# A sparse-attention and mixture-of-experts kernel: the gating's VectorE instructions regrouped, and scatters freed from an early read

## The chip, the cores and the metric
One core of one Trainium2 chip runs the whole program. The metric is device time in microseconds of an execution, as the median of several runs. Engines named here: TensorE (PE), VectorE (DVE), ScalarE (ACT), GpSimd (Pool), and SyncE (SP), which here only issues DMAs.

## The reference
Inputs q, k, v have the shape 8 x 8 x 576 x 64 (batch, head, position, feature). In heads 0 to 3 a query sees the last 32 positions up to itself; in heads 4 to 7 it sees the earlier positions of the same residue modulo 32. Scores are scaled, shifted by their row maximum, exponentiated, normalised and multiplied with v. The result is reshaped to 4608 tokens of 512 features and goes through a top-1 mixture of 8 experts:

```
logits = x @ w_gate;  e = argmax(logits);  p = softmax(logits)[e]
s = sigmoid(x @ w_output_gate)[e]
out[token] = p * s * (relu(x @ w1[e]) @ w2[e])      # w1: 512x1024, w2: 1024x512
```

## The kernel before, in words
**Stages.** Attention runs first, in 40 steps: 8 batches (b) of 5 steps (j = 0 to 4, step t = 5b + j), a step being one tile of queries of all the heads it concerns. Then comes a drain of some 20 short turns, and then the experts, one after the other, each with two layers of matmuls in a split fp32 form.

**The pipeline of a step.** The loop at the end of `attention` writes the order of the instructions by hand; each engine executes its own in that order. Step t holds: scores of tile t on PE; normalisation of tile t-4 on DVE in three instructions (`norm`, lines 345, 347, 350, the last of which writes x_t); the DMA stores of x_t and the loads of later inputs on SP; masking (`bar`) and row maximum (`top`, line 291) of tile t on DVE; transposes of tile t-2 on PE and their copy on ACT; the product with the values for tile t-3 on PE (`values`); the subtraction of the maximum on Pool (`shift`, line 306), one instruction of 128x512; transposes of x_t (`turn_x`), their copy in the next step (`evac_x`, ACT); the exponential on ACT (`expo`). `even` copies half of the local values to a shifted tile (vev), one half of the partitions on DVE and one on ACT, twice a batch, at j = 3 and j = 4 after the row maximum.

**The gating.** While batch b+1 is in attention, batch b is gated. `logits` (two halves of 288 tokens) multiplies x with both gate matrices in four strips of PE (line 413), copies to SBUF on ACT (line 417), transposes on PE (line 422) and adds the four strips on DVE (line 424). `gating` then works on tiles of 96 partitions x 6 x 8: row maximum, difference, tie-break, one-hot `oh`, its bf16 copy `ohb` (line 535), the chosen output logit, a running count of tokens per expert by triangular matmuls on PE (lines 544 to 549), the sum with the expert's base address (line 560), the product with `oh` (line 565) and its sum, the slot number as an integer (line 574), the weight (line 572). Six scatters (line 581) on Pool write token number and weight to a table in DRAM, one for each 96 tokens. Batch 7 is gated in two halves (3 scatters each), so there are nine gatings.

**The pump.** Gating and logits are generators. `pump` is called eight times a step; each call moves a generator on to its next `yield`. `yield n` makes it pass over n calls. In the drain a call goes on as long as yields are 0, in the steps it makes one move.

**The early read.** After the gating of batch 3 the kernel picks the expert with most tokens (`pick`), reads the first 256 rows of its table (`ahead`, line 470, a DMA from Pool's queue), fetches these tokens' rows by an indirect DMA on Pool and loads that expert's w1 through SP. In the drain `lead_layer` computes that expert's first layer for them on PE, one matmul at a time between the gating's work, with PSUM released by ACT (line 504) and DVE (line 506). At the end `rank` orders the experts on DVE (lines 436 to 446).

The scatters are declared free of one another (`distinct`); the framework derives every other wait from the memory that instructions read and write, the table in DRAM among it. Tiles named gp in PSUM have two buffers for all of: logits, transposes, counts, `pick`, `rank`.

## Time and profile before
| | |
|---|---|
| median of 3 runs | 645.34 us (643.64 to 649.53) |
| profiled execution | 644.6 us, of which the span of instructions is 643.0 us |
| busy: PE, DVE, ACT, Pool | 607.0, 307.2, 262.9, 188.6 us |
| DMA | 96.34 MB, mean 150 GB/s |
| mean granted clock of PE | 0.991 of 2.4 GHz |
| chain that ended last | PE 72%, issue 11%, DVE 7%, DMA 3%, ACT 3%, Pool 2% |

Busy times are means over stages that differ: the attention is the first quarter of the span, and there DVE is busy eight to nine tenths of each slice; in the experts PE is busy nine tenths and more, and DVE two to four. A time such as 63.55 is counted from the start of the span.

### The profile page before, as it was taken

The numbers are of one execution on the slowest core, as the hardware profiler recorded it, in microseconds if no ns is written. First come the engines' busy times: TensorE is split into PE (matmuls) and PEld (weight loads), VectorE is DVE, ScalarE is ACT, GpSimd is POOL, SyncE is SP. The second block draws the span as 40 slices with busy tenths as digits, with TensorE's granted clock in tenths as the row PEclk, the third lists the DMA queues.
The fourth block names the chain that finished last, engine by engine and source line by source line (L and its number), as shares of the span: only waits on it lengthen the run. The fifth ranks groups of instructions, "written<-read, shape, count | busy, mean of one in ns | idle before, by whom it ended". The sixth has DMA issues, their size and how long they took to land.

```text
span 643.0 us, 14884 instructions
## 1 busy us (share of the span) xinstructions
PE 607.0 (94%) x5909; PEld 517.0 (80%) x5909; DVE 307.2 (48%) x685; ACT 262.9 (41%) x519; POOL 188.6 (29%) x194
## 2 busy tenths in 40 slices
PE   7889898878899999999999999999999999999995
PEld 5666666656578889978998899889879988988983
DVE  4888999967672243332243234236333432532500
ACT  3766665547262153333332333243233333433410
POOL 4327555675455015011401130132015014011011
PEclk9999999979999999999999999999999999999998
DMA  8989898893524535054306342245154064161000
GB/s 315 322 283 286 286 291 274 259 340 86 181 69 135 184 103 169 1 174 143 116 2 209 125 159 67 92 126 167 35 150 129 7 208 145 36 213 48 1 22 36
DMA packets 45537, 96.34 MB, mean 150 GB/s; under 512 B 8898, under 2 KB 20438, under 8 KB 45466
## 3 DMA queue, kind: packets, MB, share of 16 engines
q1 hardware_dynamic: 36010, 71.95, 34.8%
q0 software_dynamic: 8048, 20.05, 9.6%
q10 hardware_dynamic: 1408, 3.38, 1.5%
q8 instruction: 47, 0.77, 0.5%
q14 instruction: 24, 0.20, 0.1%
HBM read 75.85 MB, written 20.35 MB: 150 GB/s over the span
## 4 chain that ended last, share of the span: by engine, by line
PE 72%; issue 11%; DVE 7%; DMA 3%; ACT 3%; POOL 2%; SPq 0%; POOLq 0%; DVEq 0%; ACTq 0%
PE hp L810 29%; PE yp L830 28%; PE tp L800 3%; PE sp L499 2%; PE yp L854 2%; PE xtp L381 2%; PE xp L332 1%; PE sp L259 1%; DVE st L291 1%; PE tp L317 1%; DVE p_t L277 1%; POOL out_dram L874 1%; PE sp L264 1%; POOL p_t L306 1%; ACT xt L396 1%
## 5 line engine op out<-in xcount | busy, mean ns | idle before, releaser
L810 PE MATMUL hp<-xh,w1l 128*128 128x256 f32 (+1 forms) x480 | 147.9, 308 | 0.0
L810 PE MATMUL hp<-xl,w1h 128*128 128x256 f32 (+1 forms) x480 | 147.8, 308 | 0.0
L810 PE MATMUL hp<-xh,w1h 128*128 128x256 f32 (+1 forms) x480 | 147.7, 308 | 0.0
L874 POOL DMA_INDIRECT out_dram<-ys,tab x36 | 38.3, 1064 | 248.9 <-ACT ys L873 237.8
L810 PEld LDWEIGHTS hp<-xh,w1h 128*128 128x128 f32 x480 | 91.0, 190 | 1.9
L810 PEld LDWEIGHTS hp<-xl,w1h 128*128 128x128 f32 x480 | 91.0, 190 | 1.9
L810 PEld LDWEIGHTS hp<-xh,w1l 128*128 128x128 f32 x480 | 90.9, 189 | 1.4
L739 DVE TENSOR_TENSOR xl<-tp,xh 128x512 fp32r<-128x512 f32 (+3 forms) x40 | 25.6, 649 | 103.3 <-ACT xh L738 103.3
L818 DVE SCALAR_TENSOR_TENSOR hlb<-hp,hhb 128x384 fp32r<-128x384 f32 (+3 forms) x64 | 33.0, 516 | 85.5 <-ACT hf L817 43.2
L815 ACT ACTIVATE hhb<-hp 128x384 fp32r<-128x384 f32 (+3 forms) x64 | 29.3, 458 | 102.8 <-PE hp L810 97.9
L830 PE MATMUL yp<-w2h,hhb 128*128 128x512 f32 (+1 forms) x176 | 71.0, 404 | 0.0
L830 PE MATMUL yp<-w2l,hhb 128*128 128x512 f32 (+1 forms) x176 | 69.6, 395 | 0.0
L830 PE MATMUL yp<-w2h,hlb 128*128 128x512 f32 (+1 forms) x176 | 69.1, 393 | 0.0
L738 ACT CAST xh<-tp 128x512 fp32r<-128x512 f32 (+3 forms) x40 | 21.8, 556 | 114.4 <-PE tp L800 114.4
L306 POOL TENSOR_TENSOR p_t<-p_t,st 128x512 f32<-128x512 f32 x40 | 46.1, 1154 | 60.0 <-DVE cum L557 16.6
L830 PE MATMUL yp<-w2h,hha 128*128 128x512 f32 x128 | 51.4, 401 | 0.0
L581 POOL DMA_INDIRECT table<-meta,dst x48 | 44.5, 927 | 22.0 <-issue 10.2
L830 PE MATMUL yp<-w2l,hha 128*128 128x512 f32 x128 | 50.2, 393 | 0.0
L830 PE MATMUL yp<-w2h,hla 128*128 128x512 f32 x128 | 50.1, 392 | 0.0
L818 DVE SCALAR_TENSOR_TENSOR hla<-hp,hha 128x256 fp32r<-128x256 f32 x56 | 23.6, 421 | 54.9 <-ACT hha L815 54.9
L155 POOL DMA_INDIRECT xg<-xd,tab x40 | 44.4, 1109 | 15.4 <-issue 12.7
L310 ACT ACTIVATE p_t<-p_t 128x512 f32<-128x512 f32 x40 | 25.2, 631 | 57.1 <-POOL p_t L306 56.9
(151 smaller groups left out, 1036.8 us busy)
## 6 DMA issues: line engine op xcount, KB each, us to landing
raw<-in_moe_w_dram SPq DMA_DIRECT2D x54, 512.0 KB
vst<-in_vs_dram SPq DMA_DIRECT2D x8, 780.0 KB
vlt<-in_vl_dram SPq DMA_DIRECT2D x16, 292.5 KB
q_t<-in_ql_dram SPq DMA_DIRECT2D x8, 576.0 KB
q_t<-in_qs_dram SPq DMA_DIRECT2D x7, 650.0 KB
xd<-x_t SPq DMA_DIRECT2D x80, 54.0 KB
xd<-x_t SPq DMA_DIRECT2D x16, 256.0 KB
raw<-in_moe_w_dram ACTq DMA_DIRECT2D x6, 512.0 KB
```

The costliest lines, as they stand in the source:

```text
L155: nc.gpsimd.indirect_dma_start(out=dst, out_offset=None, in_=src, in_offset=bass.IndirectOffsetOnAxis(ap=idx, axis=0), bounds_check=top, o ...
L306: nc.gpsimd.tensor_tensor(out=p_t, in0=p_t, in1=st, op=ALU.subtract)
L310: nc.scalar.activation(out=p_t, in_=p_t, func=AF.Exp, scale=scale)
L581: i = nc.gpsimd.indirect_dma_start(out=table[:, :], out_offset=bass.IndirectOffsetOnAxis(ap=dst[:, j:j + 1], axis=0), in_=meta[:, b * NB + ...
L738: nc.scalar.copy(out=hi, in_=src)
L739: nc.vector.tensor_tensor(out=lo, in0=src, in1=f32(hi), op=ALU.subtract)
L800: nc.tensor.transpose(out=tv[:, k, 0:m], in_=xg[0:m, 128 * k:128 * (k + 1)], identity=ident[0:m, 0:m])
L810: nc.tensor.matmul(out=hp[:, 0:n], lhsT=w[:, k, 128 * j:128 * (j + 1)], rhs=x[:, k, 0:n], start=first, stop=(k == KC - 1 and w is w1l))
L815: nc.scalar.activation(out=hh[:, j, 0:s], in_=hp[:, 0:s], func=AF.Relu)
L818: nc.vector.scalar_tensor_tensor(out=hl[:, j, 0:s], in0=hp[:, 0:s], scalar=0.0, in1=f32(hh[:, j, 0:s]), op0=ALU.max, op1=ALU.subtract)
L830: nc.tensor.matmul(out=yp[0:m, :], lhsT=h[:, j, o:o + m], rhs=w[:, j, :], start=(j == 0 and q == 0), stop=(j == FC - 1 and q == 2))
L874: i = nc.gpsimd.indirect_dma_start(out=out.rearrange("t (k d) -> (t k) d", k=k), out_offset=bass.IndirectOffsetOnAxis(ap=row, axis=0), in_ ...
```

## The change
- `logits`: the transposes and DVE's sum are replaced by a matmul with a matrix of zeros and ones (`fold`, new columns of ecst) that transposes and adds in one, and a copy on ACT.
- `gating`: `oh` is written as bf16 at once; the base addresses are added by the counting matmul, through two more rows of `cum` (filled by one small ACT copy at step 3); the sum of the slot numbers is written as an integer directly. The order is new.
- `pump` has a ninth call, number 9, between normalisation and masking, and a yield can name the call by number. For batches 0 to 5 the gating's instructions that read two tensors from SBUF are at call 9 (`MID`), its reductions at calls 3 to 6; for batches 6 and 7 the yields are counts as before, all of them 0 within `gating`.
- `even`: DVE's copies stand between normalisation and masking, at j = 4 and at j = 0 of the next batch (for batch 7 both at j = 4); ACT's stay before the exponential of these steps.
- The scatters are declared independent of the early read. `pick` and the transposes of `ahead` are tied to calls.

```diff
-                nc.vector.tensor_reduce(
-                    out=ls[b][:, HB * hf:HB * (hf + 1), :],
-                    in_=lv.rearrange("p j (c e) -> p j e c", c=KC)[:, :, 0:2 * E, :], axis=AX.X, op=ALU.add)
-                yield 0
+                    nc.tensor.matmul(out=lv[:, j, :], lhsT=lg[:, QB * j:QB * (j + 1)], rhs=fold, start=True, stop=True)
+                yield spot(b, 1, 1)
+                nc.scalar.copy(out=ls[b][:, HB * hf:HB * (hf + 1), :], in_=lv)
+                yield spot(b, 1, 5)
...
+                yield spot(b, 0, MID)
+                oh = gt.tile([QB, n, E], BF16, name="oh")
                 nc.vector.tensor_tensor(out=oh, in0=ew, in1=bc(f[:, 1, :]), op=ALU.is_equal)
-                yield 0
-                ohb = gt.tile([QB, n, E], BF16, name="ohb")
-                nc.vector.tensor_copy(out=ohb, in_=oh)
-                yield 0
-                nc.vector.tensor_tensor(out=dd[:, 0], in0=oh, in1=l[:, :, E:2 * E], op=ALU.mult)
+                nc.vector.tensor_tensor(out=dd[:, 2], in0=oh, in1=l[:, :, E:2 * E], op=ALU.mult)
+                yield spot(b, 0, 3)
...
+                nc.tensor.matmul(out=pv, lhsT=tri[0:QB + 2, 1, 0:QB],
+                                 rhs=cum[:, ci, :].unsqueeze(1).to_broadcast([QB + 2, n, E]), start=False, stop=False)
...
-                nc.vector.tensor_tensor(out=dd[:, 0], in0=pv.rearrange("p (j e) -> p j e", j=n),
-                                        in1=ec(ebase), op=ALU.add)
...
-                nc.vector.tensor_tensor(out=dd[:, 0], in0=dd[:, 0], in1=oh, op=ALU.mult)
...
-                nc.vector.tensor_reduce(out=f[:, 6, :], in_=dd[:, 0], axis=AX.X, op=ALU.add)
...
-                nc.vector.tensor_copy(out=dst, in_=f[:, 6, :])
+                yield spot(b, 0, MID)
+                nc.vector.tensor_tensor(out=cum[0:QB, ci + 1, :], in0=cum[0:QB, ci, :], in1=s8, op=ALU.add)
...
+                yield spot(b, 0, 3)
+                dst = dpool.tile([QB, n], I32, name="dst")
+                nc.vector.tensor_tensor(out=dd[:, 0], in0=pv.rearrange("p (j e) -> p j e", j=n), in1=oh, op=ALU.mult)
+                yield spot(b, 0, 4)
+                    nc.vector.tensor_reduce(out=dst, in_=dd[:, 0], axis=AX.X, op=ALU.add)
...
                     distinct(i, scatters)
+                    for r in early:
+                        tc.declare_no_dep(i.ins, r.ins, reason="the slots read were all given by earlier batches")
                     yield 3
...
-            def pump():
+            def pump(at=None):
                 clock[0] += 1
                 k = clock[0]
                 for c in chains:
-                    if k >= c[1]:
+                    if at in c[2] if at and c[2] else k >= c[1]:
...
-                pump()
+                pump(1)
                 at(norm, 4, 1)
-                pump()
+                pump(2)
                 at(norm, 4, 2)
...
+                pump(9)
+                shifted = ((0, 1) if b == B - 1 else (0,)) if j == 4 else (1,) if b and j == 0 else ()
+                for h in shifted:
+                    even(t // NS - (j == 0), nc.vector, h, 0)
                 at(bar, 0)
```

The scatters of a batch start three calls after the weight's reciprocal, and follow each other every fourth call (`yield 3`), before as after.

## Rows read from the trace of the kernel before

**Rows 1.** Windows, cut at the shift's starts of steps 5, 10, 21, 26, 33, 39.

```profile
core 0: us, PE busy (x) PEld busy (x) DVE busy (x) ACT busy (x) POOL busy (x), PEclk, DMA share, GB/s
...
23.13:39.64 16.51, 15.77 (x383) 12.04 (x384) 13.38 (x28) 12.90 (x27) 5.82 (x6) 1.00 0.93 306
...
81.91:100.48 18.57, 16.28 (x391) 12.46 (x391) 17.05 (x49) 11.55 (x26) 11.18 (x12) 1.00 0.90 283
...
127.64:153.83 26.19, 22.60 (x478) 17.61 (x471) 20.28 (x55) 14.45 (x33) 16.55 (x16) 0.87 0.75 259
153.83:198.40 44.57, 38.60 (x301) 29.32 (x300) 29.15 (x96) 20.88 (x41) 21.72 (x22) 1.00 0.34 106
```

**Rows 2.** Chain that ended last, steps 26 and 27: start, us, what.

```profile
100.69 0.91 DVE ohb L535
...
104.92 5.34 DMA hla<-in_kl_dram
```

**Rows 3.** VectorE's groups in 81.91 to 100.48: count, busy us, mean ns, idle before.

```profile
L565 DVE TENSOR_TENSOR dd<-dd,oh 96x48 f32<-96x48 f32 x1 | 1.1, 1053 | 0.0
...
L535 DVE CAST ohb<-oh 96x48 bf16<-96x48 f32 x1 | 0.9, 911 | 0.0
...
L424 DVE TENSOR_REDUCE l<-gp 96x48 f32<-96x192 f32 x2 | 0.7, 354 | 1.0 <-PE gp L422 0.9
...
L560 DVE TENSOR_TENSOR dd<-gp,ecst 96x48 f32<-96x48 f32 x1 | 0.2, 195 | 0.0
...
L574 DVE CAST dst<-f 96x6 int32<-96x6 f32 x1 | 0.2, 158 | 0.0
```

**Rows 4.** PE's group of the logits' transposes in the same stretch.

```profile
L422 PE MATMUL gp<-ident,lg 128*96 128x128 f32 x6 | 1.0, 272 | 0.0
```

**Rows 5.** Timeline of Pool, two steps of one batch: start, us, instruction, idle before.

```profile
63.34 1.08 POOL L306 TENSOR_TENSOR p_t<-p_t,st 128x512 f32<-128x512 f32 x1 [0.46 <-DVE f L529]
67.41 1.04 POOL L306 TENSOR_TENSOR p_t<-p_t,st 128x512 f32<-128x512 f32 x1 [3.00 <-DVE cum L557]
...
72.69 0.92 POOL L581 DMA_INDIRECT table<-meta,dst  x1 [0.16 <-DVE x_t L350]
73.91 0.93 POOL L581 DMA_INDIRECT table<-meta,dst  x1 [0.30 <-issue]
```

**Rows 6.** Timeline of VectorE at the same times.

```profile
63.55 0.91 DVE L535 CAST ohb<-oh 96x48 bf16<-96x48 f32 x1
...
67.47 1.05 DVE L565 TENSOR_TENSOR dd<-dd,oh 96x48 f32<-96x48 f32 x1
...
73.98 0.68 DVE L230 COPY vev<-vlt 64x1040 f32<-64x1040 f32 x1
```

**Rows 7.** Timeline of Pool around the early read (tabe) and the next steps.

```profile
125.53 0.60 POOL L470 DMA_DIRECT2D tabe<-table  x1 [0.56 <-issue]
127.64 1.39 POOL L306 TENSOR_TENSOR p_t<-p_t,st 128x512 f32<-128x512 f32 x1 [1.52 <-DVE dst L574]
131.82 0.95 POOL L581 DMA_INDIRECT table<-meta,dst  x1 [2.79 <-DVE rs L345]
...
134.03 1.05 POOL L306 TENSOR_TENSOR p_t<-p_t,st 128x512 f32<-128x512 f32 x1
...
138.80 1.06 POOL L306 TENSOR_TENSOR p_t<-p_t,st 128x512 f32<-128x512 f32 x1
```

**Rows 8.** Timeline of VectorE in the drain: gating around x_t, and the ranking.

```profile
160.14 0.69 DVE L350 TENSOR_TENSOR x_t<-xp,rs 128x512 f32<-128x512 f32 x1
160.74 0.22 DVE L553 TENSOR_REDUCE s<-oh 96x8 f32<-96x48 f32 x1
...
161.93 0.17 DVE L574 CAST dst<-f 96x6 int32<-96x6 f32 x1
...
176.49 0.22 DVE L436 COPY cnt<-gp 128x8 f32<-128x8 f32 x1
...
178.44 0.17 DVE L446 CAST erank<-rk 128x8 int32<-128x8 f32 x1
```

**Rows 9.** Timeline of PE: the lead layer's wait for its PSUM.

```profile
175.76 0.48 PE L499 MATMUL sp<-xe,raw 128*128 128x256 f32 x1 [0.78 <-DVE hla L506]
```

More of the change, by code (lines that the diff above doesn't have):

```diff
@@ L114, in setup @@
         nc.sync.dma_start(out=xd[N:N + 1, :], in_=zrow)
-    wts, eidx, ebase, rord = (ecst[:, i, :] for i in range(4))
-    cum = const.tile([QB, 2 * B - HALVED + 1, E], BF16, name="cum")
-    nc.gpsimd.memset(cum[:, 0, :], 0.0)
+    wts, eidx = (ecst[:, i, :] for i in range(2))
+    fold = ecst[:, 5:7, :].rearrange("p a e -> p (a e)")
+    NC = 2 * B - HALVED + 1
+    cum = const.tile([QB + 2, NC, E], BF16, name="cum")
+    nc.gpsimd.memset(cum[0:QB, 0, :], 0.0)
     dpool = ctx.enter_context(tc.tile_pool(name="dpool", bufs=3))
@@ L141, in attn_moe_kernel @@
     hs = []
-    scatters = []
+    scatters, early = [], []
+    assert EH <= EB * S // E
     raws, xgs = {}, {}
@@ L404, in attention @@
             ls = {}
+            MID = 9
+            spot = lambda b, n, p: (n, p) if b < B - 2 else n
             def logits(b, hf):
@@ L434, in rank @@
                 cp = ps_g.tile([128, 512], F32, name="gp")
-                nc.tensor.matmul(out=cp[:, 0:E], lhsT=tri[0:QB, 1, :], rhs=cum[:, 2 * B - HALVED, :], start=True, stop=True)
+                nc.tensor.matmul(out=cp[:, 0:E], lhsT=tri[0:QB, 1, :], rhs=cum[0:QB, 2 * B - HALVED, :], start=True, stop=True)
                 nc.vector.tensor_copy(out=cnt, in_=cp[:, 0:E])
@@ L450, in pick @@
                 cp = ps_g.tile([128, 512], F32, name="gp")
-                nc.tensor.matmul(out=cp[:, 0:E], lhsT=tri[0:QB, 1, :], rhs=cum[:, EB, :], start=True, stop=True)
+                nc.tensor.matmul(out=cp[:, 0:E], lhsT=tri[0:QB, 1, :], rhs=cum[0:QB, EB, :], start=True, stop=True)
                 yield 1
@@ L469, in ahead @@
                 src = table.rearrange("(e s) w -> e s w", e=E)[bass.ds(expert(0, nc.gpsimd), 1), 0:EH, :]
-                nc.gpsimd.dma_start(out=tabe, in_=src.rearrange("o (p c) w -> p (o c) w", p=128))
+                early.append(nc.gpsimd.dma_start(out=tabe, in_=src.rearrange("o (p c) w -> p (o c) w", p=128)))
                 for c in range(4):
@@ L478, in ahead @@
                 for c in range(EH // 128):
+                    yield 0, 2
                     tp = ps_g.tile([128, 512], F32, name="gp")
@@ L559, in gating @@
-                dst = dpool.tile([QB, n], I32, name="dst")
-                nc.vector.tensor_tensor(out=dd[:, 0], in0=pv.rearrange("p (j e) -> p j e", j=n),
-                                        in1=ec(ebase), op=ALU.add)
-                yield 0
+                yield spot(b, 0, 5)
+                nc.vector.tensor_reduce(out=f[:, 3, :], in_=dd[:, 2], axis=AX.X, op=ALU.add)
+                yield spot(b, 0, 6)
+                nc.scalar.activation(out=f[:, 4, :], in_=f[:, 3, :], func=AF.Exp, scale=-1.0)
@@ L568, in gating @@
                                                op0=ALU.add, op1=ALU.mult)
-                yield 0
-                nc.vector.tensor_reduce(out=f[:, 6, :], in_=dd[:, 0], axis=AX.X, op=ALU.add)
-                yield 0
+                yield spot(b, 0, 3)
+                dst = dpool.tile([QB, n], I32, name="dst")
+                nc.vector.tensor_tensor(out=dd[:, 0], in0=pv.rearrange("p (j e) -> p j e", j=n), in1=oh, op=ALU.mult)
+                yield spot(b, 0, 4)
+                with nc.allow_low_precision(reason="one slot's number among zeros, written as an integer"):
+                    nc.vector.tensor_reduce(out=dst, in_=dd[:, 0], axis=AX.X, op=ALU.add)
@@ L572, in gating @@
+                yield spot(b, 0, 5)
                 nc.vector.reciprocal(out=meta[:, tcols, 1].bitcast(F32), in_=f[:, 5, :])
-                yield 0
-                nc.vector.tensor_copy(out=dst, in_=f[:, 6, :])
                 if ci == 2 * B - HALVED - 1:
@@ L577, in gating @@
                 if ci == EB - 1:
-                    chains.append([pick(), clock[0] + 1])
+                    chains.append([pick(), 0, (2,)])
                 yield 2
@@ L674, in attention @@
                 at(turn_x, 4)
-                pump()
-                pump()
-                for h in ((0,) if b and j == 3 else (1,) if b and j == 4 else (0, 1) if t == 4 else ()):
-                    even(b, nc.scalar, h, 1)
-                    even(b, nc.vector, h, 0)
+                pump(3)
+                pump(4)
+                for h in shifted:
+                    even(t // NS - (j == 0), nc.scalar, h, 1)
                 at(expo, 0)
@@ L682, in attention @@
                     wipe(*WIPES[t])
+                if t == 3:
+                    nc.scalar.copy(out=cum[QB:QB + 2], in_=ecst[QB:QB + 2, 2, :].unsqueeze(1).to_broadcast([2, NC, E]))
                 if t + 1 < len(WARM):
                     warm(WARM[t + 1])
-                pump()
-                pump()
+                pump(5)
+                pump(6)
                 if live(XL) and (t - XL) % NS > 2:
-                    chains.append([logits((t - XL) // NS, (t - XL) % NS - 3), 0])
-                pump()
-                pump()
+                    chains.append([logits((t - XL) // NS, (t - XL) % NS - 3), 0, None])
+                pump(7)
+                pump(8)
                 t += 1
@@ L711, in attention @@
                 if live(4) and (t - 4) % NS > 2:
-                    chains.insert(0, [logits((t - 4) // NS, (t - 4) % NS - 3), clock[0] + 1])
+                    chains.insert(0, [logits((t - 4) // NS, (t - 4) % NS - 3), clock[0] + 1, None])
                 fill(FT[2][k] if k < 4 else FD[2])
```

57 lines of the change are left out of this document (22 added, 35 removed).

## The prediction

> **What bounds the kernel now.** I read the windows first, cut at the starts of the Pool engine's shift (line 306), which runs once in each of the 40 attention steps and so marks them. Five steps make a batch. In the batch before any gating work runs, the five steps take 16.51 us, with PE busy 15.77 (95%), VectorE 13.38, the DMA engines 0.93 at 306 GB/s. In a batch with gating the same five steps take 18.57 us: VectorE 17.05 (92%), PE 16.28 (88%), DMA 0.90 [rows 1]. So the bound moves from PE to VectorE when gating starts, and the room under VectorE is small: the next bound stands at 16.5 us. The chain of waits agrees: in the steps with gating it runs through VectorE's gating and here and there through an input transfer [rows 2]. From 198.4 us to the end of the span, 444.6 us, only the experts run, which the change does not touch; it can only start them earlier. Between lie the last six steps (26.19 us for what takes 22 elsewhere) and the drain (44.57 us) [rows 1].
>
> **VectorE's share of a batch.** Removed outright: two reductions of the logits (2 x 0.354 us), the bf16 cast (0.911), the slot base's addition (0.195), the integer cast (0.158). The product at line 565 stays, with its 1.053 us falling to the 0.2 of a gating instruction that runs freely [rows 3]. Sum: 0.71 + 0.91 + 0.20 + 0.16 + 0.85 = 2.83 us; nothing is added on VectorE, so its 17.05 falls to 14.2. Why 0.911 and 1.053 are waits and not work: the cast starts at 63.55 and ends at 64.46, just behind Pool's shift (63.34 to 64.42); the product starts at 67.47 and ends at 68.52, behind the shift of 67.41 to 68.45 [rows 5, 6]. Moving what reads two SBUF tensors between normalisation and masking takes it out of that stretch, as long as the shift is then over. The two value copies per batch (0.68 each [rows 6]) move too; I cost that at nothing, since they keep their length and only trade places with idle time.
>
> **What the others gain or lose per batch.** PE: the six transposes (0.272 each, overlapped; 1.0 us in all [rows 4]) become six matmuls of 16 columns. No such shape is in the trace; bounded by zero and by the transposes, I take half, so PE needs 16.28 - 0.5 = 15.8 us. At the 95% which it reached unhindered that is 16.6 us a batch, at today's 88% it is 18.0. ACT takes over two small copies; were they as long as its mean instruction in that batch (11.55 us over 26 [rows 1], 0.44), it would be busy 12.4 of 17 us, so that is hidden, and if it weren't it would cost 0.9. The DMA engines move 283 GB/s x 18.57 us = 5.26 MB per batch; at the 306 GB/s they did in the faster batch that takes 17.2 us. Pool keeps 6 scatters and 5 shifts, but their order changes. There are nine calls of the pump per step instead of eight, a scatter still goes out every fourth call, and calls 1, 2 and 9 stand before the shift: the six scatters fall 1, 3, 2 between successive shifts, where they were 2, 2, 2. An interval with three Pool DMAs took 4.77 us (134.03 to 138.80: a fetch and two scatters [rows 7]), against 3.71 for a mean step. That late shift, and with it exponentials, transposes and any two-input instruction caught behind it, I price at half of the excess, 0.5 us a batch. There is also a new wait on PE: the fold matmul of a batch's first half needs the PSUM buffer that the product with the running counts frees, and that product now comes after the row maximum; behind it in PE's queue are a logits matmul and the next scores. From zero to 1 us a batch; I take 0.2.
>
> So the batch period: 16.6 (PE) to 17.2 (DMA) plus 0.5 to 0.7 of bunching: **17.3 us**, 3.46 a step, between the ends 16.51 and 18.57, which are both rows. From step 10 to step 33 (39.64 to 127.64, 23 steps, 88.0 us [rows 1, 7]) that is 79.6, a gain of **8.4 us**.
>
> **The early read.** A scatter stood on Pool from 129.03, when the shift that starts at 127.64 ended, to 131.82; the early read of the table had been issued at 125.53. The next shift came at 134.03, 6.39 us after its predecessor instead of 3.71 [rows 7]. The declaration takes that wait away: 2.7 us. Next late is the row fetch: it must still wait for the read, but it comes two steps after it, as the first fetch does now. It shares an interval with three scatters at step 35, 1.05 + 4 x 1.22 (the pitch of two scatters [rows 5]) = 5.9 us of Pool, 2.4 more than the period. So the last six steps take 6 x 3.46 + 2.4 = 23.2 against 26.19: **3.0 us** gained. PE's granted clock, a mean of 0.87 there [rows 1], might recover too; I count nothing for it.
>
> **The drain.** There the pump runs on until a nonzero yield, and the whole gating is now emitted in one go. Batch 6: x_t of step 41 (160.14 us) has eight gating instructions ahead of it now; after the change all fifteen. Ten follow it now, from 160.74 to 162.10; eight of them remain and go ahead of it, 1.36 x 8/10 = 1.1 us, and with them the wait for ACT's sigmoid, an estimate of 0.4 (two engine changes of about 0.2); PE's next value products wait for x_t. Batch 7: the ranking, 176.49 to 178.61 (2.1 us on VectorE), now stands before the first PSUM release of the lead layer instead of after it, and PE, which waited 0.78 us for that release, would wait up to 2.1 more [rows 8, 9]. Against it stand the casts, bases and integer casts of three gatings, 3 x 0.5 us. Sum between 0 and +4.5; I take **+2.5 us**, as both losses lie on PE's path.
>
> **Sum.** 644.6 (the profiled execution: span 643.0 and 1.6 around it) - 8.4 - 3.0 + 2.5 = 635.7. That execution is 0.7 us under the median of 645.34, so I put the forecast at 636.
>
> **A rule that speaks against the moved copies.** At 73.91 a scatter started on Pool and took 0.93 us with a value copy of VectorE (73.98, 0.68) over it [rows 5, 6], against 0.92 for the scatter before it (72.69), which had none; so I charge nothing for copies that meet scatters. The Trainium skill, SBUF — State Buffer, section "SBUF: two separate sides", says that a VectorE fp32 SBUF-to-SBUF copy keeps GpSimd from writing the descriptors of its own DMAs. By that rule two copies a batch would stretch two scatters by up to 0.68 each, 6.3 us over 4.6 batches, and the forecast would be 642; the overlapped row does not bear it out, and I give it 2 in 100, inside rival two.
>
> **Rivals.**
> *One: PE is the only bound left.* The period falls to the 16.51 of the gating-free batch, and bunching and the drain cost nothing: 23 x 3.302 = 75.9 (-12.1), 6 x 3.302 + 2.4 = 22.2 (-4.0): 628.5. For it: VectorE would be at 14.2 of 16.5, little more than the 13.38 it had then. Against it: DMA at 5.26 MB in 16.5 us is 319 GB/s, above what any such batch shows.
> *Two: the gain is mostly eaten.* Input transfers (one of 5.34 us is on the chain already [rows 2]) or the PSUM wait hold the period at 18.2 (-4.3), the scatter's wait merely passes to the fetch, which stands in the same Pool queue and needs the same read (0; here the change doesn't do what it says), the drain loses 2.5: 642.8.
> *Three, slower: Pool's bunching.* The three scatters make one interval of 4.77 us; the shift behind them then meets the two-input gating instructions at their new place and holds each set for a full 1.05 us, a second step of 3.71 + 1.05. With three other steps at 3.71: 20.65 a batch, 4.13 a step, 95.0 for 23 steps (+7.0), the early read still gaining 2.7 and the drain losing its 4.5: 653.4. It decides from the point where a late shift starts before those instructions do: counted from the preceding shift's start, VectorE gets there after a step and a normalisation, 3.46 + 0.69 [rows 8] + two short instructions of about 0.17 = 4.5, and Pool after its shift and three scatters, 1.05 + 3 x 1.22 = 4.7. So it is close, and VectorE is ahead.
>
> **Chances.** What this kernel's measurement can tell from no change is about 1%: 638.9 to 651.8 counts as the same. Forecast 0.46 (own range 631 to 641, a quarter of it above 638.9), one 0.24, two 0.20, three 0.10. Faster 0.34 + 0.24 = 0.58, same 0.12 + 0.20 = 0.32, slower 0.10. The range 627 to 646 takes in the forecast, one and two and leaves out three and the tails.
>
> **What would show it.** In the changed profile a batch of five shifts near 17.3 us with VectorE about 14.2; no VectorE instruction of gating at 0.9 or 1.05 us (if there is one, the late shift caught it); no Pool wait of over 2 us behind the early read; the fetch's idle time next to zero; the drain from the last shift to the first expert product at 47 us. A period at 18 or more with PE waiting on the gp buffers or DMA share at 0.95 makes the forecast wrong one way; a period under 16.8 the other.

## The result and the profile after

The changed kernel takes 654.0 us (median of 4 runs, 651.64 to 654.95) against 644.49 for the kernel before beside it: ratio 1.0137 [1.0102, 1.0172]. It is slower by 9.5 us. The profiled execution took 653.9 us, its span is 652.3.

The windows of the changed kernel, cut at the same shifts as [rows 1]: steps 5 to 9, 24 to 28, 33 to 38, and the drain with step 39.

```profile
core 0: us, PE busy (x) PEld busy (x) DVE busy (x) ACT busy (x) POOL busy (x), PEclk, DMA share, GB/s
22.98:40.52 17.54, 17.54 (x404) 13.60 (x398) 13.55 (x30) 12.88 (x28) 5.22 (x6) 0.90 0.90 288
92.04:110.61 18.57, 16.61 (x395) 12.98 (x396) 16.36 (x44) 11.83 (x28) 10.78 (x11) 1.00 0.89 283
126.48:152.40 25.92, 20.24 (x449) 15.59 (x439) 19.30 (x52) 14.46 (x35) 14.01 (x15) 0.93 0.70 245
152.40:207.44 55.04, 44.05 (x318) 33.81 (x317) 26.78 (x84) 23.08 (x46) 24.47 (x24) 0.91 0.28 84
```

Read against [rows 1]: a batch with gating still takes 18.57 us. Steps 33 to 38 gained 0.27, all 29 steps from 10 on 2.3. The drain takes 55.04 us instead of 44.57, with the granted clock at 0.91 instead of 1.00. The experts take 444.9 us as before (444.6). So the account of the 9.3 us between the two spans is short: +0.9 up to step 10, -2.3 to step 39, +10.5 in the drain, +0.3 behind it. (The +0.9 is not the change's: steps 5 to 9 took 17.54 us here, at a granted clock of 0.90, and 16.74 in another profile of the same program, e12 below.)

**What held VectorE in a batch.** Pool first, then VectorE beside it, in one batch of the changed kernel (timeline, as [rows 5, 6]).

```profile
96.66 0.92 POOL L574 DMA_INDIRECT table<-meta,dst  x1 [0.15 <-issue]
97.89 0.92 POOL L574 DMA_INDIRECT table<-meta,dst  x1 [0.31 <-issue]
99.11 0.92 POOL L574 DMA_INDIRECT table<-meta,dst  x1 [0.30 <-PE xtp L384]
100.05 1.05 POOL L309 TENSOR_TENSOR p_t<-p_t,st 128x512 f32<-128x512 f32 x1
```

```profile
99.99 1.19 DVE L525 TENSOR_TENSOR dd<-l,f 96x48 f32<-96x48 f32 x1
...
103.86 0.72 DVE L534 TENSOR_TENSOR oh<-ew,f 96x48 bf16<-96x48 f32 x1
...
108.15 0.17 DVE L557 TENSOR_SCALAR f<-f 96x6 f32<-96x6 f32 x1 [0.54 <-ACT f L554]
```

The three scatters put the shift so late that it starts with the gating's difference (`dd`, line 525), which then ends behind it, after 1.19 us instead of 0.2. The next shift (103.46 to 104.51) catches the one-hot (`oh`). The third line is a wait that the old order didn't have: the sigmoid's exponential stands on ACT behind the attention's. In the two batches ahead of this one the difference runs freely, and the instruction behind it (the tie-break, `ew`, line 527) is held, as these two rows of VectorE and Pool show:

```profile
61.96 1.74 DVE L527 SCALAR_TENSOR_TENSOR ew<-dd,ecst 96x48 f32<-96x48 f32 x1
62.57 1.06 POOL L309 TENSOR_TENSOR p_t<-p_t,st 128x512 f32<-128x512 f32 x1
```

Its row starts 0.61 us ahead of the shift's, behind three scatters, and ends 0.07 us behind it, at 63.70. Over steps 14 to 28 (three batches) the groups of VectorE sum this up; columns as [rows 3]:

```profile
L527 DVE SCALAR_TENSOR_TENSOR ew<-dd,ecst 96x48 f32<-96x48 f32 x3 | 3.7, 1233 | 0.1
L534 DVE TENSOR_TENSOR oh<-ew,f 96x48 bf16<-96x48 f32 x3 | 2.6, 869 | 0.0
L525 DVE TENSOR_TENSOR dd<-l,f 96x48 f32<-96x48 f32 x3 | 1.6, 524 | 0.0
```

Freely running, each takes 0.2 us, so (3.7 + 2.6 + 1.6 - 1.8) / 3 = 2.0 us a batch go to waiting for Pool. In the kernel before it was 1.6 (the cast and the product of [rows 3]). The wait has only moved to other instructions. The Trainium skill, SBUF — State Buffer, section "SBUF: two separate sides", says that VectorE instructions with two SBUF inputs and GpSimd's share a port pair that one of them holds for a whole instruction; the ends of these rows agree (the difference at 101.18, its shift at 101.10), while the start of the row at 61.96 shows that being first does not always keep VectorE's instruction out of the wait. The moved value copies cost the scatters nothing: 18 of them took 0.929 us on average, 0.924 before, and one that ran under a copy (93.24, the copy from 93.23 to 93.97) took 0.92. So that section's other statement, on descriptors, stays unsupported by this kernel.

**PE's fold** saves nothing against [rows 4]:

```profile
L427 PE MATMUL gp<-ecst,lg 128*96 128x16 f32 x12 | 1.2, 226 | 0.0
```

Twelve of them are recorded in the batch where six are emitted, 1.2 us for the 1.0 of six transposes.

**The early read**, as [rows 7]: the wait of 2.79 us is gone.

```profile
125.87 0.59 POOL L473 DMA_DIRECT2D tabe<-table  x1 [2.78 <-PE gp L418]
126.48 1.06 POOL L309 TENSOR_TENSOR p_t<-p_t,st 128x512 f32<-128x512 f32 x1
130.79 1.04 POOL L309 TENSOR_TENSOR p_t<-p_t,st 128x512 f32<-128x512 f32 x1 [3.25 <-DVE dd L562]
131.99 0.96 POOL L574 DMA_INDIRECT table<-meta,dst  x1 [0.15 <-DMA xd<-x_t]
133.25 1.05 POOL L158 DMA_INDIRECT xg<-xd,tabe  x1 [0.30 <-issue]
134.33 1.05 POOL L309 TENSOR_TENSOR p_t<-p_t,st 128x512 f32<-128x512 f32 x1
...
140.33 1.05 POOL L309 TENSOR_TENSOR p_t<-p_t,st 128x512 f32<-128x512 f32 x1
```

The next shift comes 4.31 us after its predecessor, where it came after 6.39, and the one behind it after 3.54 instead of 4.77: 3.3 us gained. The four intervals that follow give 3.0 back: 6.00 us with the fetch and three scatters in it (4.74 before), 3.40 (2.65), 3.76 (3.90) and 4.91 (3.74). The new order alone is enough to remove the wait. The first scatter behind the read now comes 6.1 us after it, and e8 below, which has the new order without the declaration, shows no wait at that scatter either (0.15 us idle).

**The drain.** Three waits of PE that the drain of before doesn't have at these places, then VectorE ahead of the last of them, as [rows 8, 9]:

```profile
160.93 0.18 PE L542 MATMUL gp<-oh,tri 96*96 96x48 bf16 x1 [1.35 <-DVE oh L534]
163.34 0.40 PE L335 MATMUL xp<-vev,pt 128*32 128x130 f32 x1 [1.48 <-DVE x_t L353]
...
181.74 5.38 PE L502 MATMUL sp<-xe,raw 128*128 128x256 f32 x12 [2.40 <-DVE hla L509]
...
190.22 2.86 PE L502 MATMUL sp<-xe,raw 128*128 128x256 f32 x12 [0.62 <-DVE hla L509]
```

```profile
179.05 0.13 DVE L439 COPY cnt<-gp 128x8 f32<-128x8 f32 x1
...
180.92 0.17 DVE L449 CAST erank<-rk 128x8 int32<-128x8 f32 x1
181.00 0.68 DVE L509 SCALAR_TENSOR_TENSOR hla<-sp,hha 128x512 fp32r<-128x512 f32 x1
```

The ranking (179.05 to 181.0) is ahead of hla, and PE waits 2.40 us. Behind that wait twelve matmuls take 5.38 us, where the same twelve take 2.86 at 190.22. The windows show the clock beside it:

```profile
177.40:182.40 5.00, 1.81 (x7) 1.27 (x8) 4.00 (x19) 2.45 (x5) 3.74 (x5) 0.76 0.14 45
182.40:187.40 5.00, 5.00 (x14) 4.02 (x13) 1.55 (x2) 0.25 (x1) 2.13 (x2) 0.55 0.06 11
```

PE was busy for 1.81 of 5 us, and in the next 5 us its granted clock is 0.55, almost all of them at 1.2 GHz. In the drain of before PE's longest wait was 1.51 us (for ACT's copy of the logits), that for hla 0.78 [rows 9], and the clock stayed at 1.00. Over the whole drain PE is idle for 11.0 us instead of 6.0 and busy for 44.05 instead of 38.60: of the 10.5 us, 5.0 are idle time and 5.4 busy time. Two stretches of lowered clock (0.55 here, and 0.66 from 162.40 to 167.40, in which the second wait ends) make some 4 of the latter, an estimate: 5 us times 0.45 and 0.34.

The first two waits have a cause beside the order of the gating: its logits come late. In the changed kernel ACT's copy of the fold's result stands behind the copies of x; in the kernel before VectorE sums the transposes itself. VectorE's row maximum of batch 6, changed kernel and then before:

```profile
159.73 0.20 DVE L523 TENSOR_REDUCE f<-l 96x6 f32<-96x48 f32 x1 [1.13 <-ACT l L429]
```

```profile
157.91 0.20 DVE L520 TENSOR_REDUCE f<-l 96x6 f32<-96x48 f32 x1
```

PE's fold had started at 156.83, the transposes of before at 156.95: 2.90 us until the row maximum against 0.96. x_t then starts at 162.50, against 160.14 [rows 8].

### The profile page after: what moved, and what is told of

Same layout as the page of the kernel before. It is cut to its first block, busy times and chain, and to the rows that moved or that the text cites. A ratio compares the mean times of both kernels' runs of the same rounds, so it can differ in the third digit from the quotient of the medians.

```text
span 652.3 us, 14949 instructions
## 1 busy us (share of the span) xinstructions
PE 612.4 (94%) x5957; PEld 524.0 (80%) x5957; DVE 300.6 (46%) x642; ACT 265.8 (41%) x536; POOL 185.5 (28%) x194
## 4 chain that ended last, share of the span: by engine, by line
PE 63%; issue 16%; DVE 7%; POOL 6%; DMA 4%; ACT 2%; POOLq 0%; SPq 0%; DVEq 0%
PE hp L814 26%; PE yp L834 25%; PE tp L804 2%; POOL p_t L309 2%; DMA q_t<-in_qs_dram 2%; DVE st L294 2%; POOL table L574 2%; PE xtp L384 2%; PE yp L858 1%; POOL out_dram L878 1%; PE tp L320 1%; DMA xd<-x_t 1%; PE sp L267 1%; PE sp L502 1%; PE xp L335 1%
## 5 line engine op out<-in xcount | busy, mean ns | idle before, releaser
L309 POOL TENSOR_TENSOR p_t<-p_t,st 128x512 f32<-128x512 f32 x40 | 41.9, 1047 | 65.3 <-DVE st L294 16.6
```

The costliest lines, as they stand in the source:

```text
L309: nc.gpsimd.tensor_tensor(out=p_t, in0=p_t, in1=st, op=ALU.subtract)
```

## The experiments

Where the result and e9 to e12 were measured, the kernel before takes 645 us; all other runs fell on three chips where it takes 674 to 677. There steps 10 to 39 and the drain are longer in every kernel, while the experts take the same 444.3 to 444.9 us. Ratios are to the kernel before on the same chip at the same time. Running the unchanged change again (e12) moved the start of step 39's shift by 1.9 us, the drain's length by 1.8 and steps 14 to 28 by 0.7; smaller differences of the last two columns tell nothing.

| run | before, us | ratio, 95% | steps 14 to 28 | drain |
|---|---|---|---|---|
| before, profiled | | | 56.7 | 44.6 |
| the change | 644.5 | 1.0137 [1.0102, 1.0172] | 56.1 | 55.0 |
| e12 the change again | 645.3 | 1.0121 [1.0088, 1.0153] | 56.8 | 56.9 |
| e9 ranking later | 645.3 | 1.0087 [1.0055, 1.0119] | 56.1 | 50.7 |
| e10 batch 6 in chunks | 645.3 | 1.0128 [1.0096, 1.0159] | 55.9 | 54.8 |
| e11 fewer operations, no fold | 645.3 | 0.9969 [0.9951, 0.9986] | 56.9 | 46.6 |
| e4 before + declaration | 674.3 | 1.0002 [0.9954, 1.0050] | 66.6 | 58.1 |
| e1 chunks | 674.3 | 1.0053 [1.0021, 1.0084] | 68.3 | 58.0 |
| e2 last copies | 674.3 | 1.0125 [1.0084, 1.0165] | 71.3 | 64.6 |
| e3 scatter pairs | 674.3 | 0.9961 [0.9924, 0.9998] | 59.5 | 65.2 |
| e17 scatter pairs again | 677.1 | 0.9947 [0.9918, 0.9976] | 60.7 | 63.9 |
| e5 chunks, pairs | 677.5 | 0.9887 [0.9812, 0.9962] | 61.3 | 61.3 |
| e6 as e5, sigmoid early | 677.5 | 0.9918 [0.9879, 0.9957] | 59.5 | 63.7 |
| e7 fewer operations alone | 677.5 | 1.0053 [1.0014, 1.0092] | 68.8 | 58.5 |
| e8 change, no declaration | 677.5 | 1.0158 [1.0071, 1.0246] | 72.3 | 64.5 |
| e13 pairs, ranking later | 677.2 | 0.9923 [0.9891, 0.9954] | 60.6 | 61.4 |
| e14 pairs, chunks, ranking | 677.2 | 0.9860 [0.9810, 0.9909] | 60.9 | 60.1 |
| e15 as e14, no fold | 677.2 | 0.9922 [0.9894, 0.9950] | 63.0 | 61.5 |
| e16 as e15, last copies | 677.2 | 0.9959 [0.9921, 0.9997] | 61.7 | 61.1 |
| e18 as e14 again | 677.1 | 0.9881 [0.9850, 0.9912] | 64.4 | 61.1 |

### The drain: e1, e2, e9, e10, e12

e1, batches 6 and 7 gated in four chunks again (three yields of `gating`):

```diff
-                yield spot(b, 0, 3)
+                yield spot(b, 1, 3)
                 nc.scalar.activation(out=dd[:, 1], in_=dd[:, 0], func=AF.Exp)
...
-                yield spot(b, 0, 3)
+                yield spot(b, 1, 3)
                 s8 = gt.tile([QB, E], F32, name="s8")
...
-                yield spot(b, 0, MID)
+                yield spot(b, 1, MID)
```

> The changed kernel, with batches 6 and 7 gated in four chunks again (yields of 1 after the tie-break, after the chosen logit and after the sigmoid), nothing else. Before, the drain from the last shift to the first expert product took 44.6 us, after 55.0. Theory (the one-go emission puts x_t of step 41 behind the whole gating and the ranking ahead of the lead layer's PSUM release, PE idles twice and its granted clock falls): 5 to 8 us of the 10.4 come back, the run at 646 to 649, and no stretch of the drain at a granted clock near 0.6. Rival (the loss is the two value copies of the last step, or the two-input waits): 1 us or less, 653.

Drain 58.0 against 64.6 in the run beside it that kept the single go (e2), and the same as the 58.1 of before's order: by this run the gating in one go is the drain's loss. The size is not so sure, as e5 and e6 below have the same drain and take 61.3 and 63.7 on another chip. e10 has the chunks for batch 6 alone (`spot(b, b == B - 2, 3)` and so on).

> The changed kernel with batch 6 alone gated in four chunks in the drain (a yield of 1 after the tie-break, the chosen logit and the sigmoid); batch 7 as in the change. Theory 1 (the ranking ahead of hla makes most of the drain's loss): ratio 1.010 to 1.014, 0 to 2 us better than the change. Rival (batch 6's gating ahead of x_t makes it): about 5 us better, ratio 1.006; with both batches in chunks it was 1.0053.

Nothing gained: 1.0128 against 1.0121 for the change on the same chip. That points to batch 7, with the reserve that e1 ran on a slower chip. e9 moves the ranking alone:

```diff
                 nc.vector.reciprocal(out=meta[:, tcols, 1].bitcast(F32), in_=f[:, 5, :])
-                if ci == 2 * B - HALVED - 1:
-                    rank()
                 if ci == EB - 1:
                     chains.append([pick(), 0, (2,)])
                 yield 2
+                if ci == 2 * B - HALVED - 1:
+                    rank()
```

> The changed kernel with the ranking (L439 to L449) taken out of the last gating's single go: it stands one pump call later, just ahead of the last three scatters, so the lead layer's first PSUM release (hla L509) goes ahead of it on VectorE. Theory 1 (the drain loses 6 to 10 us, and most of it is this: PE waits 2.40 us for hla behind the ranking, and the granted clock falls to 0.62 after that wait, which costs the layer's first matmuls another 2.5 us): ratio to before 1.006 against 1.0137 for the change, drain (last shift to first expert product) about 5 us shorter. Rival (the loss lies earlier, where batch 6's x_t stands behind fifteen gating instructions): ratio within 0.003 of the change's.

Drain 50.7, ratio 1.0087: 2 to 3 us of the 9 given back (against e12 and against the result; the intervals of e9 and e12 overlap, so the time alone leaves this open, and the profile carries it). In e9's timeline hla stands ahead of the ranking, PE waits 0.91 us, and the twelve matmuls take 2.86:

```profile
180.84 2.86 PE L502 MATMUL sp<-xe,raw 128*128 128x256 f32 x12 [0.91 <-DVE hla L509]
```

The windows of e9 at the same place keep the clock at 1.00:

```profile
178.38:183.38 5.00, 3.70 (x19) 3.03 (x18) 3.90 (x19) 1.61 (x4) 3.75 (x5) 1.00 0.19 63
183.38:188.38 5.00, 4.78 (x21) 3.56 (x20) 3.26 (x4) 4.37 (x5) 2.22 (x2) 1.00 0.05 7
```

Of the 4.4 us by which its drain is shorter than the change's, 1.5 are wait (2.40 to 0.91) and 2.5 are clock (5.38 to 2.86). Other profiles repeat it: in the seven with the ranking ahead of hla and batch 7 in one go (the change, e2, e3, e8, e10, e12, e17) the wait is 2.40 to 2.43 us and the twelve matmuls take 4.48 to 5.49; with the ranking behind it (e9, e13) the wait is 0.91 to 0.93 and they take 2.86. The wait alone doesn't decide the clock, though. In e5 they took 2.86 behind a wait of 2.18 us, in e7 4.54 behind one of 0.78:

```profile
206.30 2.86 PE L502 MATMUL sp<-xe,raw 128*128 128x256 f32 x12 [2.18 <-DVE hla L509]
```

```profile
206.76 4.54 PE L499 MATMUL sp<-xe,raw 128*128 128x256 f32 x12 [0.78 <-DVE hla L506]
```

And e14 and e18, one program (below), differ: a wait of 0.85 us and 2.86, then 2.19 and 4.54. About 6 us of the drain's loss stay in e9: PE's waits of 1.34 and 1.48 us on batch 6's gating and x_t are as in the change. e10 should have shown them; in its profile the granted clock stood at 0.50 for the second five microseconds of the drain, where the change's had 1.00. So did it in e12, which is the change itself: the place of the lowered clock differs from one execution to the next, and e10's profile can't settle batch 6's part.

> The changed kernel as it is, on the chip of the three others, so that their drains and batches can be laid beside its own. Every theory: ratio to before 1.010 to 1.017; drain 6 to 11 us longer than that of the kernels with before's order.

e2 undid one more move, both value copies of batch 7 at step 39:

```diff
-                shifted = ((0, 1) if b == B - 1 else (0,)) if j == 4 else (1,) if b and j == 0 else ()
+                shifted = ((0,) if j == 3 else (1,) if j == 4 else (1,) if j == 0 else ()) if b == B - 1 else (0,) if j == 4 else (1,) if b and j == 0 else ()
```

> The changed kernel, with the value copies of batch 7 alone at steps 38 and 39 instead of both at step 39. Theory (both copies on ACT, 2.0 us, stand before the last exponential, and PE waits 1.5 us behind them): 1 to 2 us back, 652. If the drain's loss starts with this delay: 5 us or more. If ACT had room: nothing.

No effect is seen (1.0125; the change itself was not run on this chip).

### The declaration: e4, e8

e4 is the kernel before with the `declare_no_dep` lines of the change, e8 the change without them.

> The kernel before, with the scatters declared independent of the early read and nothing else. Theory: the wait of 2.8 us on Pool goes, the shift of step 34 comes 2 to 2.7 us earlier, the run at 642. Rival (the wait passes to the fetch, or batch 7's transfers set the pace of steps 33 to 39): 644.5, unchanged.

> The changed kernel with the scatters waiting for the early read again. In the changed kernel the first scatter after the read stands 6.1 us behind it anyway (125.87 and 131.99). Theory (the new order alone had already taken the wait away, the declaration is worth nothing): 1.0137 as the change, Pool idle under 1 us before that scatter. Rival (the declaration is worth what was forecast): 2 to 3 us slower than the change, 1.018.

No gain of the declaration is seen in either order (1.0002; 1.0158 beside the change's 1.0121 to 1.0137 on another chip). This isn't the same as nothing: e4's interval reaches down to 0.9954, 3.1 us, and e8 has two runs. In e4's profile the wait is gone (0.16 us) and the shift behind it comes after 3.84 us instead of 6.39; the two intervals that follow take 7.49 and 4.69.

### Fewer operations: e7, e11

e7 is the kernel before with the fold, the bf16 one-hot, the base in the counting matmul and the integer sum, in before's order. e11 is the same without the fold: transposes and VectorE's sum stay.

> The kernel before with the fewer operations alone: fold matmul and ACT copy, bf16 one-hot, base in the counting matmul, integer sum; order, calls, value copies and the early read's wait as before. Theory (VectorE bound the period, and the order is what took the gain): VectorE busy 14.2 to 14.5 us per batch, a period of 17 to 17.5, step 39 comes 5 to 7 us earlier, 0.990. Rival (transfers or Pool hold 18.57): period and time unchanged, 1.000.

> The kernel before with fewer VectorE instructions (bf16 one-hot, base by the counting matmul, integer sum) but with its own transposes and VectorE's sum of the four strips kept; order, calls and copies as before. The same with the fold and its ACT copy gave 1.0053. Theory A (the fold makes that loss: VectorE waits 4.0 us in three batches for the copy of l on ACT): ratio 0.990 to 0.997. Rival B (the removed instructions were in slack, the loss is another): 1.002 to 1.006.

Removing VectorE's work shortened no batch here. The windows of steps 14 to 28, the kernel before, then e11, both on chips of 645 us:

```profile
55.77:112.47 56.70, 49.02 (x1170) 37.48 (x1169) 51.65 (x151) 34.76 (x79) 33.91 (x33) 1.00 0.89 284
```

```profile
55.81:112.68 56.87, 48.60 (x1168) 37.56 (x1160) 49.02 (x141) 35.23 (x79) 34.13 (x34) 1.00 0.90 287
```

VectorE loses 2.6 us of work, the three batches take 0.2 more. Where e11's gain (0.9969) lies isn't shown: its profile has steps 33 to 38 in 23.7 us instead of 26.2 and the drain in 46.6 instead of 44.6, while two profiles of the same program (the change and e12) differ by 1.3 and 1.8 us there. With the fold (e7, on a chip of 677) VectorE falls from 53.0 (e4) to 48.1, and the time rises; a wait that only the fold has stands at the row maximum:

```profile
L520 DVE TENSOR_REDUCE f<-l 96x6 f32<-96x48 f32 x2 | 0.4, 200 | 4.0 <-ACT l L426 4.0
```

That row covers 80 to 130 us. e7 and e11 ran on different chips, as did e4 and e7, so how much the fold itself costs isn't separated.

### The scatters: e3, e17, e5, e6, e13, e14, e18

e3 and e17 tie the scatters of batches 0 to 5 to calls 3 and 7, so that two at most fall between two shifts:

```diff
-                yield 2
+                yield spot(b, 2, (7,))
                 for j in range(n):
...
-                    yield 3
+                    yield spot(b, 3, (3, 7))
```

> The changed kernel, with the scatters of batches 0 to 5 at calls 3 and 7, so 1, 2, 2, 1 of them stand between shifts instead of 1, 3, 2. Theory (the shift that comes late behind three scatters blocks the two-input instructions at their new place): the difference and the one-hot fall from 1.19 and 0.72 us to 0.2, the period of five steps from 18.57 to 17 to 17.5, step 39 comes 5 to 7 us earlier, the run at 647 to 649. Rival (input transfers hold the period at 18.57, the same figure in both kernels): the two instructions fall to 0.2 us and the period stays, the run at 654.

> The changed kernel with the scatters of batches 0 to 5 at calls 3 and 7 alone, once more for its batch period, in the hope of a chip where the kernel before takes 645 us. There, theory A (the three scatters between two shifts hold the batch at 18.57): steps 14 to 29 in 52 to 53.5 us against 56.1 for the change, VectorE under 15 us a batch, ratio 0.999 to 1.005. Rival B (ACT's new waits hold it): 55 to 56 us, ratio 1.010 to 1.014. On a chip of 675 us: as before, 59 to 61 us, ratio 0.993 to 0.999, and the question of the period stays open for the others.

On chips of 675 us steps 14 to 28 take 59 to 62 us with pairs in seven profiles (63 and 64 in e15 and e18), 68 to 72 with three scatters (e1, e2, e8), and the ratio falls from 1.0125 (e2) to 0.9961 beside it. But it is not by the mechanism of the expectations. There the two-input instructions ran freely with three scatters too, as the groups of VectorE in e8 show (steps 14 to 28), with another wait in their place:

```profile
L348 DVE TENSOR_SCALAR rs<-xp 128x8 f32<-128x8 f32 x15 | 2.2, 150 | 10.6 <-remote 9.5 <-PE xp L335 1.1
...
L527 DVE SCALAR_TENSOR_TENSOR ew<-dd,ecst 96x48 f32<-96x48 f32 x3 | 0.6, 204 | 0.1
```

"Remote" is a releaser that the profile can't name. PE stalls at the same time (109.07 to 111.86 is one of these waits; the scatters run from 107.48 to 110.86), in the middle of its score matmuls:

```profile
110.33 0.36 PE L267 MATMUL sp<-kbs,q_t 64*64 64x64 f32 x4 [0.40 <-issue]
111.77 0.47 PE L267 MATMUL sp<-kbs,q_t 64*64 64x64 f32 x12 [1.09 <-issue]
```

The windows of steps 14 to 28, e8 and then e17, show the price, clock and all:

```profile
53.30:125.57 72.27, 61.72 (x1186) 47.07 (x1186) 45.20 (x130) 36.59 (x84) 32.42 (x33) 0.86 0.77 245
```

```profile
53.18:113.87 60.69, 53.04 (x1187) 41.17 (x1187) 45.20 (x130) 35.82 (x84) 32.44 (x34) 1.00 0.86 280
```

VectorE's work is equal, 45.2 us or 15.1 a batch; PE's grows from 53.0 to 61.7 with the clock at 0.86. That is 8.7 of the 11.6 us; 2.9 more are PE's idle time. What the stall waits for is open. In the new order the longer batches go with the third scatter, but a third scatter isn't what it takes: e4 and e7, in before's order with two at most between shifts, take 66.6 and 68.8 us on these chips. In e4 the clock is at 1.00, and waits of the same kind stand at the masking:

```profile
L277 DVE TENSOR_TENSOR p_t<-sp,mask 128x512 f32<-128x512 f32 x6 | 4.1, 686 | 7.2 <-remote 5.0 <-PE tp L317 2.2
```

The edit moves the scatters within the step as well as thinning them, so the count and the place aren't separated. Whether pairs would shorten the batch on a chip of 645 us is open too, since no run with them fell on one.

e5 joins e1 and e3, and e6 adds to it the sigmoid's exponential ahead of the attention's:

```diff
+                nc.vector.tensor_reduce(out=f[:, 3, :], in_=dd[:, 2], axis=AX.X, op=ALU.add)
                 s8 = gt.tile([QB, E], F32, name="s8")
...
                 nc.vector.tensor_reduce(out=f[:, 2, :], in_=dd[:, 1], axis=AX.X, op=ALU.add)
-                yield spot(b, 0, 5)
-                nc.vector.tensor_reduce(out=f[:, 3, :], in_=dd[:, 2], axis=AX.X, op=ALU.add)
-                yield spot(b, 0, 6)
                 nc.scalar.activation(out=f[:, 4, :], in_=f[:, 3, :], func=AF.Exp, scale=-1.0)
```

> The changed kernel with both repairs: the drain's gating in four chunks and the scatters at calls 3 and 7. Against the kernel before on their own chip, the chunks alone gave 1.0053 and the scatters alone 0.9961, where the change gave 1.0137. Theory (two separate causes): the two gains add, 0.988. Rival (both act through the same thing, the scatters' place in Pool's queue or transfers as the floor of the attention): no better than 0.996.

> The kernel of the run before with the chosen logit's sum and the sigmoid's exponential moved ahead of the step's big exponential in ACT's queue (calls 3 and 4 instead of 5 and 6). In the changed kernel VectorE waits 0.54 us for it in each batch between normalisation and masking (line 557). Theory (that wait is on the path): it goes, and the run is 2 to 3 us (0.3 to 0.5%) under the run before. Rival (PE or transfers would fill the time anyway): the wait goes and the time stays.

e5 beats the kernel before on its chip, where e8, the change but for the declaration, is slower than it (two runs). In e6 the wait for the sigmoid is gone and no gain over e5 is seen; e5's interval is wider than the 0.3 to 0.5% asked about, so that wait's price stays open. e13 joins pairs and e9, e14 adds the chunks, e18 is e14 again.

> The changed kernel with two undos: scatters of batches 0 to 5 tied to calls 3 and 7 (1, 2, 2, 1 of them between shifts, never three), and the ranking after the wait for the scatters. Where the kernel before takes 645 us (there the change alone has 18.6 us a batch and ratio 1.012 to 1.014): theory A (the three scatters between two shifts hold the batch at 18.57, since the late shift blocks the two-input instructions) expects no ew, oh or dd of gating over 0.3 us, VectorE under 15 us a batch, 17.3 to 17.6 us a batch, attention 4 to 6 us shorter, ratio 0.998 to 1.002. Rival B (the period is held by ACT's new waits, the sigmoid and the late copies of x, whatever the shift does): 18.3 to 18.6 us a batch and ratio 1.006 to 1.009, as with the ranking alone. On a chip where the kernel before takes 675 us: 0.990 to 0.994 by A, 1.006 or more by B.

> As the one before, and both last batches gated in four chunks in the drain. Theory A: the drain 2 to 5 us shorter than with the ranking alone, within 2 us of the 44.6 of before; ratio 0.990 to 0.996. Rival (what is left of the drain's loss comes from the fold and its copy on ACT, and from both value copies on ACT at step 39, not from the gating in one go): no more than 1 us better than the run before it.

> Scatters at calls 3 and 7, the ranking behind the first PSUM release, and both last batches in four chunks, once more. On a chip where the kernel before takes 645 us: by theory A 0.988 to 0.995 (periods as in the run beside it, drain of 46 to 48 us); by B about 1.000. On a chip of 675 us: 0.983 to 0.990, as it was (0.986).

0.9923, then 0.986 and 0.9881: the last two, of one program, are the lowest ratios, 7 to 10 us under the kernel before on chips of 677 us, though not apart from e5's 0.9887. None of these has run on a chip of 645 us. The drain is 2 to 3 us over the 58.1 of e4.

e15 puts the transposes and VectorE's sum back into e14, e16 adds e2's edit to that.

> As the one before, with the transposes and VectorE's sum of the four strips in place of the fold and its ACT copy. With before's order the fold lost 0.8% (1.0053 with it, 0.9969 without). If it loses as much here: 0.004 to 0.008 under the run before it. Rival (with the two-input instructions unblocked VectorE has no room problem either way, and the ACT copy costs nothing): within 0.002 of it.

> As the one before, with the value copies of batch 7 one at step 38 and one at step 39, as in the kernel before, and not both at 39, where ACT's two took 2.01 us ahead of the last exponential. If that costs what stood there: 1 us (0.0015) better and PE's idle time before step 39's transposes gone; a run of this move alone showed nothing (1.0125 against 1.0121 to 1.0137).

Neither gains. In the new order and on that chip the fold is no loss.

## Why the prediction was wrong

It said 636 us (627 to 646), with a chance of 0.10 for slower by over 1%; measured 654.0. Two steps failed most: VectorE was taken for what holds a batch, and the drain's loss was sized at 2.5 us. By terms, forecast and then measured in the profile: steps 10 to 32 -8.4 and -2.0, steps 33 to 38 -3.0 and -0.3, the drain +2.5 and +10.5, the rest 0 and +1.1. The steps, in its order:

**What bounds a batch.** The step "So the bound moves from PE to VectorE when gating starts" failed. VectorE was busy for 92% of the stretch, but part of that busy time was waiting for Pool (1.6 us a batch). e11 took 0.9 us a batch from it, and the batch kept 18.9 us. A busy share says how full an engine is, not that the others wait for it; [rows 2] showed an input transfer of 5.34 us on the chain, and it was read as an exception. What does hold the batch at 18.6 us on chips of 645 us isn't settled, and the profiles speak for two things. DMA was at a share of 0.91 to 0.93 and 297 to 305 GB/s over steps 14 to 28 in the four kernels with the new order there (the change, e9, e10, e12), close to the 0.93 and 306 of the batch without gating, and transfers take 7 and 12 us of the chain in the change and e10. In e9 and e12, with batches as long, the chain of these steps holds no transfer at all; it runs through VectorE, Pool's scatters and shift (10 to 13 us of 56), the caught one-hot and the sigmoid, as these pieces of e12 show (start, us, what):

```profile
98.89 0.92 POOL table L574
...
99.82 1.07 POOL p_t L309
...
103.48 0.87 DVE oh L534
...
107.78 0.11 ACT f L554
```

No run changed the transfers, and none freed these pieces on a chip of 645 us.

**VectorE's share.** The sum of -2.83 us was right where nothing blocked: 53.0 to 45.2 over three batches (e4 to e17) is -2.6 a batch. On the chip of the result it was 51.65 to 50.44, -0.4 a batch, since 2.0 us of blocking came back.

**Bunching.** Priced at 0.5 us a batch, it cost VectorE 2.0 us of blocking on the chip of the result. Rival three had said when: "Pool after its shift and three scatters", 4.7 against VectorE's 4.5, "So it is close, and VectorE is ahead". Pool's figure was met: in the three batches the shift started 4.59 to 4.60 us after its predecessor. VectorE's difference started 4.53 after it in one batch, with a lead of 0.06 us, and was caught all the same; in the two others it started at 3.73 and 3.76 and ran freely, and the tie-break behind it, with a lead of 0.61 to 0.63, took 1.74 to 1.75 us and ended with the shift. So a lead of 0.6 us was not enough, and who starts first, by which rival three was judged, isn't what decided. The price of such a catch should have been in the forecast's own sum. Rival three's 653.4 us meets the measured time by chance only: its losses were to lie in the steps, and those got 2 us shorter.

**PE's gain and ACT's copies.** The fold's 0.5 us was not there. The waits on ACT (the sigmoid 0.54 us a batch on VectorE, the copies of x up to 1.6 us on PE in steps 14 to 28) weren't foreseen; what they cost is not shown. ACT's new copies, put at nothing since ACT has room over a batch, hold batch 6's gating up in the drain: 1.9 us later behind PE than before (2.90 against 0.96). Room on average says nothing of one copy's place in the queue.

**The early read.** The wait went, the 3.0 us did not come. The reading of the wait as a delay of its step held: that interval fell from 6.39 to 4.31 us. So did the price of the crowded one (5.9 forecast, 6.00 measured). What failed is that all the others were put at 3.46 us: they took 3.40 to 4.91, and the last of them has both value copies of batch 7 on ACT beside it. The declaration, to which the wait was credited, isn't even needed in the new order (e8).

**The drain.** Both mechanisms were named and both seen: x_t behind the whole gating, the ranking ahead of the first PSUM release. The size was not: +2.5 with a range to +4.5, measured +10.5. Neither figure comes out of the stated terms, which add up to 3.6 of loss (1.1, 0.4 and 2.1) and 1.5 of gain. The failed term is PE's waits counted at their own length: idle time grew by 5.0 us, and PE's busy time by another 5.4, some 4 of them (the estimate above) because the granted clock fell. Of the ranking's part (4.4 us) 1.5 were the wait and 2.5 the clock behind it. The 1.5 us of removed operations didn't show as a gain either: e11, which removes them in before's order, has a drain of 46.6 us against 44.6. About 6 us are accounted for only in part: two waits of 1.3 to 1.5 us on batch 6, with the late logits ahead of them (the sigmoid's wait, put at 0.4, was 0.20), and windows of lowered clock behind them. No run on a chip of 645 us separates the late logits from the gating in one go.

## What to carry to other kernels

Before pricing removed work at its busy time, take some out and see whether the period moves; busy time in which an instruction is held until another engine's ends isn't work, and something else may hold the period at the same length. Where a scheduler runs "until the next yield", every yield that becomes zero moves all later instructions of that generator ahead of its neighbours: follow each queue past which they move, the last stage above all. A wait on PE can cost more than its own length, by a stretch of lowered clock behind it: price it as a range, and look at the granted clock of more than one profile, since the same program doesn't lose it in the same places each time.

## What the hardware showed that was not expected

- A wait of 2.40 us on PE, with PE busy for 1.81 of 5 us, was followed by 5 us at a granted clock of 0.55, and twelve matmuls took 5.38 us instead of 2.86. With a wait of 0.91 us at the same place the clock stayed at 1.00, and so it did behind one of 1.51 us in the drain of before. The length of the wait alone doesn't tell: in e5 the same matmuls took 2.86 us behind a wait of 2.18, in e7 4.54 behind one of 0.78.
- An instruction of VectorE with two SBUF inputs, 0.2 us when it runs freely, took 1.74 us although its row starts 0.61 us ahead of Pool's shift: it ended 0.07 us behind it (63.70 and 63.63).
- The same program took 645 us in two measurements and 674 to 677 in four others, on three chips, with equal experts (444.3 to 444.9 us). On the latter, waits of VectorE and ACT have no releaser in the profile (e4 and e8 above), which no profile on a chip of 645 us shows over steps 14 to 28, and PE stalls in the middle of a run of matmuls (e8). Why the chips differ is not known.
